# Reading a K and V cache in rows 64 KB apart: two successive loads share an 8 MB region and take alternate 32 KB pieces

## The chip, the core and the metric

The kernel runs on one core of a Trainium2 chip; the other cores are idle. The metric is device time in microseconds (us), lower is better. Executions of one kernel agree within about 0.3%. A verdict needs a difference of 2% outside a 95% interval. All ratios below are the mean time of one kernel's fast runs over that of the other's in the same rounds, so they are not quite the ratio of the medians quoted beside them.

## The reference, cut to what matters

One token attends to a cache of 65536 keys in each of 32 heads; a small gated MLP on the same token is mixed in. The two caches are 512 MB each (32 x 65536 x 128 x 2 bytes), so reading them is nearly all there is to do.

```python
H, Sk, Dh = 32, 65536, 128                 # x is [1, 1, 512], everything bf16
q = (x @ wq).reshape(1, 1, H, Dh)...       # one query per head
scores = einsum("bhqd,bhkd->bhqk", q, k_cache) * Dh ** -0.5
p = softmax(scores, axis=-1)
o = einsum("bhqk,bhkd->bhqd", p, v_cache)
a = o... @ wo
return g * a + (1 - g) * b                 # b: the MLP, g: a gate
```

The order of the keys within a head is of no account, as long as K and V agree on it: softmax and the sum over the keys do not see it.

## The kernel before

A load ("job") brings 4 MB: a quarter of one head's keys, 128 partitions with 128 keys (32 KB) each. There is a ring of four such slots in SBUF. K loads and V loads alternate in it. The SP engine issues every load as soon as the slot that it goes to is free.

```python
P = 128; CB_MAX = 128; NSLOT = 4           # CB = 128 keys per partition and load, NCH = 4 loads per head
ring = sb("ring", [P, NSLOT, SLOT], BF16)  # SLOT = 128 * 128 elements = 32 KB per partition

def kv_src(t, i):                          # the DRAM side of K or V load i
    h, c = divmod(i, NCH)
    return t[0, h, c * CB * P:(c + 1) * CB * P, :].rearrange("(p r) d -> p (r d)", p=P)

def pieces(job):
    ...
    src = kv_src(A_k_cache if kind == "k" else A_v_cache, i)
    dst = flat(job)[:, 0:CB * 128]
    ...
    return [(dst, src)]

def load(eng, w, job):                     # on SP, in the order of `jobs`
    i = place[job]
    if i >= NSLOT:
        for cond in free_of(jobs[i - NSLOT]):
            w(*cond)                       # the slot's old content is used up
    for n, (dst, src) in enumerate(pieces(job)):
        ...
        eng.dma_start(dst, src).then_inc(done, 16)
```

On the compute side each K load is transposed by PE (into psT) and copied by ScalarE (into KT), PE multiplies it with the query, and VectorE does a quarter of the keys itself (prod). Each V load goes to PE as weights. None of this is touched by the change.

## Time and profile before

| | before |
|---|---|
| time, median of the first 3 runs | 2563.17 us |
| bytes read | 1087.64 MB |
| PE / VectorE / ScalarE busy | 72% / 49% / 58% |
| DMA queue of the cache loads, share of 16 engines' span | 98.8% |

The lines below are from the page of the profile. The first two are the busy share of the 16 DMA engines and the rate in 40 equal slices of the span; then comes the queue that carries the loads (packets, MB, share of the engines' time), the chain of work that ended last, two groups that use the data (busy time and mean ns of one, then idle time before them and what ended it), and the loads with their size and the median time from issue to landing.

```profile
DMA  9999999999999999999999999999999999999996
GB/s 403 423 425 432 432 431 431 430 431 430 433 430 432 430 431 433 430 433 429 433 429 431 433 426 431 430 432 427 426 425 418 431 429 427 423 422 426 422 419 297
...
q1 hardware_dynamic: 37874, 1083.46, 98.8%
...
DMA ring<-in_A_k_cache_dram 66%; ACT KT L345 10%; PE psT L535 9%; PE psS L548 2%; PE psO L566 1%; ACT pcol L325 1%; DMA ring<-in_A_wq_dram 1%; PE psT L596 0%; PE psT L515 0%; POOL amx L304 0%; PE psS L508 0%; PE psO L589 0%; DVE mxs L441 0%; ACTq L205 0%; DVE sS L434 0%
...
L535 PE MATMUL psT<-ident,ring 128*128 128x128 bf16 x12288 | 1138.7, 255 | 527.6 <-DMA ring<-in_A_k_cache_dram 525.5
...
L424 DVE TENSOR_TENSOR prod<-ring,qbc 128x2048 f32<-128x2048 bf16 x256 | 586.7, 2292 | 592.1 <-DMA ring<-in_A_k_cache_dram 586.7
...
ring<-in_A_k_cache_dram SPq DMA_DIRECT2D x128, 4096.0 KB, 28.0
ring<-in_A_v_cache_dram SPq DMA_DIRECT2D x127, 4096.0 KB, 33.7
```

Reading: the DMA engines are busy in every slice but the last. PE and VectorE each sit idle for over 500 us, nearly all of it ended by a K load that landed. The chain is 66% K load. A load takes 28 to 34 us to land, although 4 MB at 431 GB/s take 9.7 us: about three loads stand in the queue at any time.

The SP queue's own waits (engine and line, what it waited for, us in total, times, longest) say who frees the slots:

```profile
SPq L205 <- DVE prod L424: 1368.2, 128, 11.8
SPq L252 <- PE psT L535: 522.0, 126, 10.7
SPq L252 <- PE psO L566: 487.1, 124, 7.3
```

SP waits 2377 us in these three lines, but for room in a queue that already holds work, so these waits cost nothing as long as the engines do not run dry.

The trace has a record of each packet. A packet here is one contiguous piece: one partition's row.

| packet | count | median ns | mean ns | us per engine, sum |
|---|---|---|---|---|
| 32 KB (K and V rows, and 128 of wq) | 32768 | 1214 | 1223.8 | 2506.4 |
| 14 KB (MLP weights) | 384 | 541 | 542.7 | 13.0 |
| 1 KB (nearly all wo) | 4097 | 46 | 50.4 | 12.9 |
| all others | | | | 15.0 |
| sum, of a span of 2563.3 us | | | | 2547.3 |

The last column is the time of all packets of that size divided by 16. It explains the time: 2547 of 2563 us are packets, so the 16 engines have next to no gaps between them. (A record does not name the engine of its packet, so this is the mean of the 16.) The fastest three quarters of the 32 KB packets lie between 1211 and 1218 ns, a rate of 27.0 GB/s per engine and 432 GB/s for 16.

### The profile page before, as it was taken

The page shows a single profiled execution, that of the slowest core. Times are in us where ns is not written, and L with a number is a line of the kernel's source. Part 1 is how long each engine was busy: PE and PEld are TensorE (multiplying, and loading weights), DVE is VectorE, ACT ScalarE, POOL GpSimd, SP SyncE. Part 2 cuts the span into 40 slices and gives each one's busy share as a digit, 9 for nine tenths or more (in the row PEclk, how much of TensorE's full clock was granted, in tenths as well). Part 3 has the DMA queues.
Part 4 walks back from the last instruction along what each step waited for, and adds up shares of the span by engine and source line. Part 5 has one row for each costly group of instructions (what it writes and reads, how often), then busy time and mean ns, then how long its engine had stood idle before and what let it go on. Part 6 is the DMA issues. An engine that isn't in the chain of part 4 may idle for free.

```text
span 2563.3 us, 88371 instructions
## 1 busy us (share of the span) xinstructions
PE 1848.0 (72%) x41279; PEld 1701.2 (66%) x41280; DVE 1259.2 (49%) x953; ACT 1484.7 (58%) x1799; POOL 42.3 (2%) x72
## 2 busy tenths in 40 slices
PE   6877777777777767776777677777766776777766
PEld 4777666666666666666766666666666666666665
DVE  2754554554455445544554454455444544455441
ACT  3766665566556655655665566556655665566552
POOL 0000000000000000000000000000000000000000
PEclk8778776777767767777676677777777777777776
DMA  9999999999999999999999999999999999999996
GB/s 403 423 425 432 432 431 431 430 431 430 433 430 432 430 431 433 430 433 429 433 429 431 433 426 431 430 432 427 426 425 418 431 429 427 423 422 426 422 419 297
DMA packets 42053, 1088.43 MB, mean 425 GB/s; under 512 B 4481, under 2 KB 8578, under 8 KB 8706
## 3 DMA queue, kind: packets, MB, share of 16 engines
q1 hardware_dynamic: 37874, 1083.46, 98.8%
q10 hardware_dynamic: 4112, 4.19, 0.5%
q8 instruction: 27, 0.44, 0.1%
q14 instruction: 40, 0.33, 0.0%
HBM read 1087.64 MB, written 0.00 MB: 424 GB/s over the span
## 4 chain that ended last, share of the span: by engine, by line
DMA 67%; PE 13%; ACT 11%; issue 9%; POOL 0%; DVE 0%; ACTq 0%; SPq 0%; POOLq 0%; DVEq 0%
DMA ring<-in_A_k_cache_dram 66%; ACT KT L345 10%; PE psT L535 9%; PE psS L548 2%; PE psO L566 1%; ACT pcol L325 1%; DMA ring<-in_A_wq_dram 1%; PE psT L596 0%; PE psT L515 0%; POOL amx L304 0%; PE psS L508 0%; PE psO L589 0%; DVE mxs L441 0%; ACTq L205 0%; DVE sS L434 0%
## 5 line engine op out<-in xcount | busy, mean ns | idle before, releaser
L345 ACT ACTIVATE KT<-psT 128x1024 bf16<-128x1024 bf16 x1536 | 1443.0, 1039 | 972.7 <-PE psT L535 969.8
L535 PE MATMUL psT<-ident,ring 128*128 128x128 bf16 x12288 | 1138.7, 255 | 527.6 <-DMA ring<-in_A_k_cache_dram 525.5
L535 PEld LDWEIGHTS psT<-ident,ring 128*128 128x128 bf16 x12288 | 912.3, 116 | 538.3 <-DMA ring<-in_A_k_cache_dram 271.7
L424 DVE TENSOR_TENSOR prod<-ring,qbc 128x2048 f32<-128x2048 bf16 x256 | 586.7, 2292 | 592.1 <-DMA ring<-in_A_k_cache_dram 586.7
L548 PE MATMUL psS<-qc,KT 128*128 128x1 bf16 x12288 | 550.8, 166 | 139.9 <-ACT KT L345 92.7
L548 PEld LDWEIGHTS psS<-qc,KT 128*128 128x128 bf16 x12288 | 467.7, 100 | 257.7 <-ACT KT L345 252.5
L426 DVE TENSOR_REDUCE sS<-prod 128x16 f32<-128x2048 f32 x256 | 585.2, 2286 | 8.7
L566 PE MATMUL psO<-pcol,ring 128*128 128x1 bf16 x16384 | 475.7, 164 | 19.9 <-issue 9.2
L566 PEld LDWEIGHTS psO<-pcol,ring 128*128 128x128 bf16 x16384 | 450.4, 99 | 24.0 <-issue 14.6
L434 DVE COPY sS<-psS 128x96 f32<-128x96 f32 x128 | 33.0, 257 | 607.2 <-PE psS L548 607.2
L325 ACT ACTIVATE pcol<-sS,nbias 128x128 bf16<-128x128 f32 x128 | 52.3, 408 | 41.7 <-POOL nbias L306 41.6
L304 POOL PARTITION_ALL_REDUCE amx<-mxs x32 | 16.1, 502 | 2137.5 <-DVE mxs L441 2137.5
L445 DVE COPY oparts<-psO 128x1 f32<-128x1 f32 x127 | 18.9, 149 | 25.2 <-PE psO L566 25.1
L306 POOL TENSOR_SCALAR nbias<-amx 128x1 f32<-128x1 f32 x32 | 24.5, 767 | 333.6 <-issue 333.6
L325 ACT ACTIVATION_READ_ACCUMULATOR pcol<-sS,nbias 128x1 f32 x128 | 26.1, 204 | 0.0
L380 DVE COPY qc<-qTb 128x1 bf16<-128x1 bf16 x128 | 19.9, 156 | 4.4
L441 DVE TENSOR_REDUCE mxs<-sS 128x1 f32<-128x512 f32 x32 | 21.7, 677 | 0.0
L332 ACT ACTIVATE qbc<-psT 128x512 bf16<-128x512 f32 x4 | 2.4, 597 | 23.1 <-PE psT L515 23.1
L596 PE MATMUL psT<-wo_sb,oTn 128*1 128x512 bf16 x31 | 11.2, 540 | 5.6 <-DVE oTn L476 5.6
L508 PE MATMUL psS<-xT,ring 128*128 128x1 bf16 x128 | 3.6, 165 | 12.3 <-DMA ring<-in_A_wq_dram 12.3
L508 PEld LDWEIGHTS psS<-xT,ring 128*128 128x128 bf16 x128 | 3.5, 104 | 12.4 <-issue 12.4
L596 PEld LDWEIGHTS psT<-wo_sb,oTn 128*1 128x1 bf16 x31 | 3.3, 110 | 12.7 <-issue 11.7
(44 smaller groups left out, 43.2 us busy)
## 6 DMA issues: line engine op xcount, KB each, us to landing
ring<-in_A_k_cache_dram SPq DMA_DIRECT2D x128, 4096.0 KB, 28.0
ring<-in_A_v_cache_dram SPq DMA_DIRECT2D x127, 4096.0 KB, 33.7
wo_sb<-in_A_wo_dram ACTq DMA_DIRECT2D x1, 4096.0 KB, 157.0
ring<-in_A_wq_dram SPq DMA_DIRECT2D x1, 4096.0 KB, 17.6
ring<-in_A_v_cache_dram SPq DMA_DIRECT2D x1, 3584.0 KB, 34.6
ring<-in_B_w_gate_dram SPq DMA_DIRECT2D x1, 1792.0 KB, 31.3
ring<-in_B_w_up_dram SPq DMA_DIRECT2D x1, 1792.0 KB, 35.5
ring<-in_B_w_down_dram SPq DMA_DIRECT2D x1, 1792.0 KB, 39.7
```

The source lines that it names most:

```text
L306: nc.gpsimd.tensor_scalar_mul(nbias[:, h:h + 1], amx[:, h:h + 1], -SCALE).then_inc(sm["s_nb"], 1)
L325: nc.scalar.activation(p_of(c), sS[:, h % NS, j * CB:(j + 1) * CB], ACT.Exp, bias=nbias[:, h:h + 1], scale=SCALE, accum_out=rsum[:, c:c + ...
L345: nc.scalar.activation(KT[:, g % NKT, :], kt_ps(g), ACT.Copy, bias=0.0).then_inc(sm[ev_of(g)[0]], 1)
L380: nc.vector.tensor_copy(qc[:, c % 2:c % 2 + 1], qTb[:, c // NCH:c // NCH + 1]).then_inc(sm[cq_of(c)[0]], 1)
L424: nc.vector.tensor_tensor(prod[:], kb, qb, ALU.mult).then_inc(sm["s_tt"], 1)
L426: nc.vector.reduce_sum(sS[:, h % NS, cc * CB + b0:cc * CB + b0 + DB], prod[:], AX_X).then_inc(sm["s_rd"], 1)
L434: nc.vector.tensor_copy(sS[:, h % NS, cc * CB:cc * CB + CBT], psS[:, c % 2, 0:CBT]).then_inc(sm["s_rc"], 1)
L441: nc.vector.reduce_max(mxs[:, h:h + 1], sS[:, h % NS, :], AX_X).then_inc(sm["s_mx"], 1)
L445: nc.vector.tensor_copy(oparts[:, c:c + 1], psO[:, c % 2, 0:1]).then_inc(sm[oc_of(c)[0]], 1)
L535: last = nc.tensor.transpose(dst[:, k * 128:(k + 1) * 128], src[:, b * 128:(b + 1) * 128], ident[:])
L548: last = mm(psS[:, c % 2, col:col + 1], KT[:, g % NKT, k * 128:(k + 1) * 128], qc[:, c % 2:c % 2 + 1], start=True, stop=True)
L566: last = mm(psO[:, c % 2, 0:1], src[:, b * 128:(b + 1) * 128], p_of(c)[:, b:b + 1], start=(b == 0), stop=(b == CB - 1))
```

## The change

The intent is to read the cache in another order in memory. Two successive loads share a region of 8 MB; partition p owns 64 KB of it and the even load takes the first 32 KB, the odd one the second. A row is still one contiguous piece of 32 KB, but rows of one load are now 64 KB apart in place of 32 KB.

```diff
         def kv_src(t, i):
             h, c = divmod(i, NCH)
-            return t[0, h, c * CB * P:(c + 1) * CB * P, :].rearrange("(p r) d -> p (r d)", p=P)
+            keys = t[0, h, c // 2 * 2 * CB * P:(c // 2 + 1) * 2 * CB * P, :]
+            return keys.rearrange("(p r) d -> p (r d)", p=P)[:, c % 2 * CB * 128:(c % 2 + 1) * CB * 128]
```

## The prediction

> **What bounds the kernel now.** The DMA engines. The profile's page gives them a busy digit of 9 in 39 of 40 slices, and a mean of 425 GB/s over a span of 2563.3 us. The compute engines are all below: PE 72%, ACT 58%, DVE 49%. The chain of waits that ended last is 66% "ring<-in_A_k_cache_dram". The SP queue's own waits show that it issues a load as soon as a slot is freed, and the issue table gives 28.0 us (K) and 33.7 us (V) from issue to landing for 4096 KB, about three times the 9.7 us that 4096 KB take at 431 GB/s: about three loads stand in the DMA queue all the time, so no engine waits for an issue. The packet records of the trace have 32768 packets of 32 KB, exactly 128 for each of 256 cache loads. Their median is 1213 ns, the first percentile too, so one engine runs at 27.0 GB/s and 16 at 432 GB/s: this is a floor of the engine, not of HBM waits. The mean is 1222.6 ns, because about 2% of the packets are slow (up to 3454 ns). The slow ones lie mostly after 1800 us, where the stretches table shows 420 to 428 GB/s in place of 431.
>
> **What the change does.** Only the source pattern of the K and V loads: a partition's 32 KB row is still one contiguous piece, but the pitch from partition to partition goes from 32 KB to 64 KB. Two successive loads then read the two halves of one 8 MB region. The built programs have the same instructions in the same order on each engine (1855 rows compared, no difference but line numbers); sizes, semaphores, slots and destinations are the same. Keys land in other columns, for K and V alike, so the softmax and the sum see the same pairs. Nothing is removed, nothing added: packets, bytes, issue costs and compute stay.
>
> **What can differ.** Only how fast HBM answers. The Trainium skill, "DMA: Bandwidth & Descriptors", section "Latency and other measured facts", reports for HBM copies of 16 KiB rows a loss at large power-of-two pitches: 207 against 214 GB/s at 512 KiB, 164 at 2 MiB. No run here shows this yet. 64 KB is an eighth of the pitch that cost 3% there, so I estimate a loss of a few tenths of a per cent at most, in a higher share of slow packets. The gain is bounded: if every packet took 1213 ns, 2048 packets per engine would save 2048 x 9.6 ns = 20 us, so about 2543 us (estimate). A gain over 2% is excluded by the engine floor: 1087.6 MB at 432 GB/s are 2517 us before head and tail.
>
> All of any packet slowdown lies on the critical path: 1% on the mean packet is about 25 us.
>
> **Prediction.** 2566 us, 8 in 10 between 2548 and 2595. Faster by over 2%: 0.01. Within 2%: 0.89. Slower by over 2%: 0.10.
>
> **What would show each step right or wrong.** Right: packet median still 1213 ns and 32768 packets of 32 KB; GB/s digits about 430 in the middle slices; landing times 28 and 34 us; unchanged counts and means in the groups of instructions. Wrong: a packet median above 1213 ns, or many more packets above 1300 ns, GB/s below 422 in the middle, with landing times up in proportion and longer PE and DVE waits for "ring<-in_A_k_cache_dram".
>
> **What would make it wrong.** Engines that read at the same time now stand twice as far apart in address; if that maps them on the same part of HBM, packets stretch and the time follows one for one (5% on the packet is 125 us). Or the slow packets after 1800 us come from the old addresses and vanish: then up to 20 us faster.

## The result, and the profile after

| | before | after |
|---|---|---|
| time, median of 4 runs each | 2563.11 us (2558.77 to 2563.19) | 2561.61 us (2560.03 to 2562.92) |
| ratio, 95% interval | | 0.9998 (0.9981 to 1.0015) |
| 32 KB packets: count, median, mean ns | 32768, 1214, 1223.8 | 32768, 1213, 1223.2 |
| 32 KB packets over 1400 ns | 424 | 386 |
| packet time per engine, of the span | 2547.3 of 2563.3 us | 2545.8 of 2560.1 us |

The change does nothing to the time. The same lines of the page, after:

```profile
DMA  9999999999999999999999999999999999999996
GB/s 403 423 427 430 432 431 433 430 432 430 431 431 431 432 430 431 433 430 430 433 430 431 431 429 429 428 428 429 430 427 425 433 426 427 422 425 429 425 425 297
...
q1 hardware_dynamic: 37874, 1083.46, 98.8%
...
DMA ring<-in_A_k_cache_dram 66%; PE psT L536 10%; ACT KT L346 10%; PE psS L549 2%; PE psO L567 1%; ACT pcol L326 1%; DMA ring<-in_A_wq_dram 1%; PE psT L597 0%; PE psT L516 0%; POOL amx L305 0%; PE psS L509 0%; PE psO L590 0%; DVE mxs L442 0%; ACTq L206 0%; DVE sS L435 0%
...
L536 PE MATMUL psT<-ident,ring 128*128 128x128 bf16 x12288 | 1143.2, 255 | 529.8 <-DMA ring<-in_A_k_cache_dram 527.9
...
L425 DVE TENSOR_TENSOR prod<-ring,qbc 128x2048 f32<-128x2048 bf16 x256 | 586.7, 2292 | 594.3 <-DMA ring<-in_A_k_cache_dram 589.0
...
ring<-in_A_k_cache_dram SPq DMA_DIRECT2D x128, 4096.0 KB, 28.0
ring<-in_A_v_cache_dram SPq DMA_DIRECT2D x127, 4096.0 KB, 33.7
```

Landing times are the same to a tenth of a us, the packet count is the same, the chain is the same 66%, and VectorE still waits 589 us for K loads (586.7 before).

### The profile page after: what moved, and what is told of

Its sections match the earlier page's. It is cut to its first block, busy times and chain, and to the rows that moved or that the text cites. A ratio compares the mean times of both kernels' runs of the same rounds, so it can differ in the third digit from the quotient of the medians.

```text
span 2560.1 us, 88371 instructions
## 1 busy us (share of the span) xinstructions
PE 1850.6 (72%) x41279; PEld 1704.9 (67%) x41280; DVE 1259.3 (49%) x953; ACT 1484.3 (58%) x1799; POOL 46.1 (2%) x72
## 4 chain that ended last, share of the span: by engine, by line
DMA 67%; PE 14%; ACT 11%; issue 9%; POOL 0%; DVE 0%; ACTq 0%; SPq 0%; POOLq 0%; DVEq 0%
DMA ring<-in_A_k_cache_dram 66%; PE psT L536 10%; ACT KT L346 10%; PE psS L549 2%; PE psO L567 1%; ACT pcol L326 1%; DMA ring<-in_A_wq_dram 1%; PE psT L597 0%; PE psT L516 0%; POOL amx L305 0%; PE psS L509 0%; PE psO L590 0%; DVE mxs L442 0%; ACTq L206 0%; DVE sS L435 0%
## 5 line engine op out<-in xcount | busy, mean ns | idle before, releaser
L425 DVE TENSOR_TENSOR prod<-ring,qbc 128x2048 f32<-128x2048 bf16 x256 | 586.7, 2292 | 594.3 <-DMA ring<-in_A_k_cache_dram 589.0
## 6 DMA issues: line engine op xcount, KB each, us to landing
ring<-in_A_v_cache_dram SPq DMA_DIRECT2D x127, 4096.0 KB, 33.7
```

The costliest lines, as they stand in the source:

```text
L425: nc.vector.tensor_tensor(prod[:], kb, qb, ALU.mult).then_inc(sm["s_tt"], 1)
```

## The experiments

A null result leaves three explanations, and the prediction had taken the first.

- **Engine floor.** A DMA engine moves 32 KB in 1213 ns, whatever the addresses; the memory has room to spare. The order in memory then does not matter until it is bad enough to eat up that room.
- **Memory order matters, but 64 KB is too small a step to show it.** A larger pitch then costs little by little.
- **The loads do not bound the kernel.** If slots or engines set the pace, faster or slower packets would be hidden.

Twelve kernels were run, each beside the kernel before on the same chip. Several read the wrong keys; the work done is the same. The comparison with the reference is of no use for seeing which keys were read.

### Fewer bytes with the same work: bytes_7_8

```diff
+            if place[job] >= 12:
+                return [(dst[:, 0:CB * 112], src[:, 0:CB * 112])]
             return [(dst, src)]
```

> From the 13th load on, each K and V load brings 7/8 of its row (28 KB in place of 32 KB); wrong result on purpose, all other work unchanged. DMA-bound theory: about 245 loads shrink by 1/8 of 9.75 us, 299 us less, so 2264 us within 1%. Rival (the engines' work or the release of slots bounds, and the memory pattern is masked by it): well under half of that gain, over 2410 us.

Measured: 2271.7 us, ratio 0.8877 (0.8855 to 0.8899). By the ratio that is 11.23% of the 2562 us that before took beside it (mean of seven runs), 288 us less. 246 loads shrank: the issue table has 121 K and 126 V loads of 3584 KB, but one of the V entries is the first piece of the last load, which is cut in two in every kernel (lines below). 246 x 8 rows per engine x the 152 ns between the median 32 KB packet of before (1214) and the median 28 KB packet of this run (1062) are 299 us. The loads bound the kernel: 96% of their saving arrives. The third explanation is out. The chain of waits and its waiting engines show where the rest goes (the issue table and the chain from the page, then the table of who waited for whom):

```profile
ring<-in_A_v_cache_dram SPq DMA_DIRECT2D x126, 3584.0 KB, 27.4
ring<-in_A_k_cache_dram SPq DMA_DIRECT2D x121, 3584.0 KB, 23.0
...
DMA ring<-in_A_k_cache_dram 37%; ACT KT L347 14%; PE psT L537 12%; PE psO L568 7%; PE psS L550 4%; ACT pcol L327 1%; POOL amx L306 1%; DMA ring<-in_A_wq_dram 1%; DVE mxs L443 1%; PE psT L598 0%; PE psT L517 0%; POOL nbias L308 0%; DVE sS L436 0%; PE psS L510 0%; PE psO L591 0%
```

```profile
DVE prod L426 <- DMA ring<-in_A_k_cache_dram: 215.5, 97, 3.7
PE psT L537 <- DMA ring<-in_A_k_cache_dram: 169.8, 88, 3.9
```

K loads fall from 66% to 37% of the chain, VectorE's waits for them from 586.7 to 215.5 us, and PE is busy for 82% of the span in place of 72%. There is not much room behind the DMA.

### A larger pitch: pitch128k, pitch512k, pitch2m, pitch4m

These widen the region that a load is spread over. At 128 KB the four loads of a head share it and the result is right. At 512 KB, 2 MB and 4 MB, 4, 16 and all 32 heads share it, and keys of different heads are mixed. Where the texts below say "the skill", they mean the row of the page that the prediction names, and the times that they work out from its figures are estimates.

```diff
-            return t[0, h, c * CB * P:(c + 1) * CB * P, :].rearrange("(p r) d -> p (r d)", p=P)
+            # pitch128k
+            keys = t[0, h].rearrange("(p r) d -> p (r d)", p=P)
+            return keys[:, c * CB * 128:(c + 1) * CB * 128]
+            # pitch512k; pitch2m has 16 heads and 64 loads in place of 4 and 16
+            g = h // 4 * 4
+            keys = t[0, g:g + 4].rearrange("h s d -> (h s) d").rearrange("(p r) d -> p (r d)", p=P)
+            n = i % 16
+            return keys[:, n * CB * 128:(n + 1) * CB * 128]
+            # pitch4m
+            keys = t[0].rearrange("h s d -> (h s) d").rearrange("(p r) d -> p (r d)", p=P)
+            return keys[:, i * CB * 128:(i + 1) * CB * 128]
```

> The change taken one step further: the four loads of a head share its 16 MB, rows 128 KB apart; the result stays right. Engine theory (a DMA engine moves 32 KB in 1213 ns whatever the addresses): packet median 1213 ns, time 2561 us within 0.3%. Memory-order theory (the pitch costs, but 64 KB is too little to show it): some loss here, 1% or more (over 2585 us).

> The largest pitch that the cache allows: rows of one load stand 4 MB apart, loads step by 32 KB. The result is wrong on purpose (keys of different heads are mixed), the work is the same. Engine theory in its pure form: 2561 us within 0.3%. Memory-order theory, with the skill's halving of HBM copies at a 4 MiB pitch: the packet mean doubles, 4000 us or more. In between if the memory has some headroom at this pitch.

> Rows of a load 512 KB apart (four heads share 64 MB; wrong result on purpose). Theory of engines in step (16 engines that read at the same offset modulo the pitch meet on the same part of the memory, and the pitch has to be large): a small loss between nothing (pitch128k) and 7.3% (pitch4m), estimate 0 to 2%, 2561 to 2612 us, packet median still 1213 ns. The skill's table of HBM copies would give 3% here, 2640 us. Theory that pitch4m is slow for another reason than a power-of-two pitch (rows of 16 or more heads touched by each load): no loss here.

> Rows 2 MB apart (16 heads share 256 MB; wrong result on purpose). Engines in step: between pitch512k and pitch4m, 2580 to 2750 us, with the slowest slices at the start, where the engines have not drifted apart yet. The skill's table for copies (164 against 214 GB/s) would give 30%, 3300 us.

| pitch | time, median us | ratio to before (95%) | packet median / mean ns | packets over 1400 ns |
|---|---|---|---|---|
| 32 KB (before) | 2563.11 | | 1214 / 1223.8 | 424 |
| 64 KB (the change) | 2561.61 | 0.9998 (0.9981 to 1.0015) | 1213 / 1223.2 | 386 |
| 128 KB | 2562.07 | 1.0003 (0.9985 to 1.0022) | 1214 / 1222.2 | 325 |
| 512 KB | 2562.28 | 1.0000 (0.9983 to 1.0016) | 1214 / 1222.3 | 381 |
| 2 MB | 2567.74 | 1.0026 (1.0009 to 1.0043) | 1213 / 1224.1 | 499 |
| 4 MB | 2757.30 | 1.0730 (1.0702 to 1.0757) | 1213 / 1299.7 | 4782 |

Kernels are compared only within the same rounds. Of the six runs of pitch4m, two (2822 and 2779 us) count as slow, being over 1.5% above the fastest; the ratio is of the other four. Their granted clocks (0.720 and 0.717) are hardly below those of the others (0.719 to 0.723), so the spread may well be this kernel's own; the mean of all six is 7.9% above the 2562 us of before. The second explanation, loss little by little, does not hold in the range of the change: up to 512 KB nothing is lost, at 4 MB 7.3%. At 2 MB it is 0.26%: the interval leaves out 1, but the mean packet of the profiled run (1224.1 ns against 1223.8) hardly shows it. The pure form of the first falls as well: an engine's packet is not independent of the addresses everywhere. At 4 MB the median packet is still 1213 ns, but one packet in seven (4782 of 32768) is over 1400 ns. The excess over 1213 ns, summed and divided by 16, grows from 22 to 178 us per engine, so 155 of the 161 us that the span of the profiled run is longer (2724.3 against 2563.3 us).

The Trainium skill, "DMA: Bandwidth & Descriptors", section "Latency and other measured facts", gives for copies between HBM tensors in 16 KiB rows 207 GB/s at a pitch of 512 KiB, 164 at 2 MiB and 103 at 4 MiB, of 214. The direction agrees, the sizes do not carry over to these loads from HBM into SBUF in 32 KB rows: 0%, 0.26% and 7.3% more time here, against 3%, 23% and 52% less rate there.

### The same distance, another remainder: pitch4m_skew

```diff
+            pitch = H * S - P * CB               # in keys: 128 partitions, each 4 MB less 32 KB
+            keys = t[0].rearrange("h s d -> (h s) d")[0:pitch, :].rearrange("(p r) d -> p (r d)", p=P)
+            n = i % (NK - 1)
+            return keys[:, n * CB * 128:(n + 1) * CB * 128]
```

> As pitch4m, but a row stands 4 MB less 32 KB after the one before it: as much memory touched by each load, rows as far apart, but no longer at the same offset modulo 4 MB (wrong result on purpose). Engines in step: the loss goes, 2561 us within 0.5%, packet mean 1223 ns, first slices 403 and 423 GB/s as before. Theory that distance or the spread over 512 MB costs: 7% slower as pitch4m, 2750 us.

Measured: 2561.01 us, ratio 0.9999 (0.9982 to 1.0015). The rates by slice, first pitch4m, then pitch4m_skew:

```profile
GB/s 313 290 334 381 396 398 395 423 421 420 405 401 419 426 417 403 418 426 427 420 406 409 414 411 414 410 425 427 419 406 392 410 411 410 398 403 420 427 387 249
```

```profile
GB/s 403 422 428 433 430 431 432 433 428 433 433 427 433 432 427 433 433 428 433 430 430 433 430 429 431 431 430 431 426 424 432 429 425 427 415 429 431 425 431 299
```

With 32 KB taken off the pitch the whole loss is gone: packet mean 1222.3 ns, 324 packets over 1400 ns. So it is neither the distance between rows nor the spread over 512 MB that costs, but that the rows of a load lie at the same remainder modulo 4 MB. (A pitch of 2 MB also gives equal remainders, modulo 2 MB, and costs 0.26%; why 4 MB costs so much more was not tested.) This agrees with the skill's advice in the same row of its table to pad such a pitch by a few KiB (it tells of +4 KiB; here it was -32 KB).

### The same bytes for all: one_row and hot4m

```diff
+            # one_row: every partition reads the same 32 KB
+            row = t[0, h, c * CB * P:c * CB * P + CB, :].rearrange("r d -> (r d)")
+            return row.unsqueeze(0).broadcast_to([P, CB * 128])
+            # hot4m: every load reads the first 4 MB of K or of V
+            return t[0, 0, 0:CB * P, :].rearrange("(p r) d -> p (r d)", p=P)
```

> All 128 partitions of a load are filled from the same 32 KB row (pitch 0; wrong result on purpose). Engine theory in its pure form (an engine's rate needs nothing of the memory): 2561 us. Engines in step: 16 engines want the same bytes at the same time, at least the loss of pitch4m, over 2750 us, unless the memory serves repeated rows from something faster.

> All 256 cache loads read the same 4 MB of K or of V; wrong result on purpose. Theory that the slow packets (over 1400 ns; 424 in before, 386 in after) are a matter of addresses: they mostly go, excess over 1213 ns falls from 22 us to under 10 us, time 2545 to 2552 us. Theory that they come from what the program does at that moment: the same clusters once per head after 1600 us, 2561 us within 0.2%.

one_row: 2560.77 us, ratio 0.9997 (0.9980 to 1.0013), with a wrong result. My expectation of a loss was wrong: 128 rows at one address do no harm, while 128 different rows 4 MB apart do. Whether repeated rows come from something faster was not looked into.

hot4m: 2562.83 us, ratio 1.0008 (0.9988 to 1.0028), 370 packets over 1400 ns and 20.4 us of excess, against 424 and 22.1 before. So the slow packets are not a matter of which addresses are read, as the last sentence of the prediction had held possible. The records say more: after 1600 us many of them come in clusters, in all three kernels of this table at nearly the same moments. (Counting as a cluster five or more slow packets less than 3 us from one to the next, 247 of the 424 of before lie in clusters, some of them earlier. The times below are on the clock of the records; the span of the profile's other tables starts at 11 us on it, so subtract 11.)

| kernel | some clusters of slow packets, us |
|---|---|
| before | 1750, 1830, 1909, 1989, 2066, 2145 |
| after | 1752, 1830, 1909, 1986, 2065, 2144 |
| hot4m | 1751, 1829, 1908, 2066, 2146 |

### Once per head, or once per eight loads: loads2m

```diff
-CB_MAX = 128
+CB_MAX = 64
```

> The kernel before with loads of half the size (2 MB, rows of 16 KB), so 16 loads to a head in place of 8. The result stays right. Where do the slow packets come from, which all kernels so far show every 8 loads, 78 us, after 1600 us? If they belong to the DMA queue (a count of loads): every 8 loads, so about every 39 us. If they belong to the program (something done once per head): every 16 loads, 78 us. Time: 8 ns more for each of 2048 extra packets per engine (the packet records give 46 ns for 1 KB, 159 for 4 KB, 309 for 8 KB, so about 8 ns fixed), 16 us more, 2578 us within 1%.

Measured: 2593.45 us, ratio 1.0122 (1.0105 to 1.0139). Clusters at 1782, 1862, 1942, 2101 and 2181 us: one in 80 us, that is 16 loads, not 8. With bytes_7_8, where a head takes less time, they are 70 us apart, still one per head. So they belong to something that the program does once per head, and not to a count of loads in the DMA queue. What that is was not found; all of it together is at most the 22 us of excess, 0.9%. The time is 0.6% above the 2578 us that were expected (32 us more than before, not 16): the slices of the first 130 us are slow (361 and 320 GB/s), with slots of half the size.

### Smaller pieces: piece2k

```diff
+            keys = t[0, h, c // 2 * 2 * CB * P:(c // 2 + 1) * 2 * CB * P, :]
+            keys = keys.rearrange("(p n two r) d -> p n two (r d)", p=P, two=2, r=8)
+            return keys[:, :, c % 2, :]
...
-            dst = flat(job)[:, 0:CB * 128]
+            dst = flat(job)[:, 0:CB * 128].rearrange("p (n x) -> p n x", x=1024)
...
-                cut = (CB - TAIL) * 128
+                cut = (CB - TAIL) // 8
```

> The change with smaller pieces: two slots share the 8 MB region and take alternate 2 KB of each partition's 64 KB, in place of alternate 32 KB. The result stays right. Engine theory (about 8 ns fixed and 37.6 ns per KB for each packet, from the packets of 1, 4 and 8 KB in the trace of before): 2 KB take 84 ns, 32 KB 1340 ns in place of 1213, so 2048 x 127 ns = 260 us more, 2821 us within 2%. Memory theory (the same bytes within 8 MB in another order, served alike): 2561 us.

Measured: 2834.72 us, ratio 1.1068 (1.1049 to 1.1086); expected were 2821 us within 2%. The page's queue line:

```profile
q1 hardware_dynamic: 529266, 1083.46, 103.9%
```

524288 packets of 2 KB have a median of 88 ns, and their times overlap a little (103.9%), so the rate is the safer number: 386 GB/s in the middle slices, against 431. The result is right and the region is the 8 MB of the change; only the length of a piece differs. It is the contiguous length that has a price here, about 9 ns for each further packet (273 us for 15 x 2048 of them per engine), and the change kept that length.

### Who meets whom at 4 MB: pitch4m_stagger and pitch4m_stagger2

Rows at the same remainder may clash between engines that work in step, or within one engine's own sequence of rows. Slow first slices in pitch4m (313, 290, 334, then around 400 and over) looked like engines that start in step and drift apart. To build a stagger from the start, 15 small loads of 15, 14, ... 1 rows were added to pitch4m, meant to give some engines more to do than others; how the rows of a load are shared among the engines is not in the records.

```diff
+            for job in jobs[:2]:                 # pitch4m_stagger2 only
+                load(sp, w, job)
+            at = 0
+            for n in range(15, 0, -1):
+                sp.dma_start(KT[at:at + n, 0, :], A_k_cache[0, 0, 0:n * GB, :].rearrange(
+                    "(p r) d -> p (r d)", p=n)).then_inc(sm["s_junk"], 16)
+                at += n
-            for job in jobs:
+            for job in jobs[2:]:                 # pitch4m_stagger: jobs
                 load(sp, w, job)
...
                 w("tdone", g + 1)
+                w("s_junk", 240)                 # ScalarE, before it writes KT
```

> As pitch4m (wrong result on purpose), but 15 small loads of 15, 14, ... 1 rows of 2 KB go into the queue first[...]; the addresses of the cache loads are those of pitch4m. Theory of engines in step (different engines meet on the same part of the memory): with the engines apart from the start, the first 250 us run at over 390 GB/s in place of 275 to 335, and the loss shrinks from 7.3% to under 3%, under 2640 us (the small loads themselves cost about 8 us). Theory that one engine's own successive rows clash, or that distance costs: same slow start, 2750 us.

> pitch4m_stagger again, mended: there the small loads went into an empty queue, one every 0.48 us, while 2 KB take 0.084 us, so the engines had caught up before the next one and the stagger was never built. Here they are issued behind wq and the first K load, into a full queue (about 20 us of work, 7.2 us of issue)[...] (wrong result on purpose, addresses of pitch4m). Engines in step: from the second K load on over 390 GB/s, which the stretches from 100 to 250 us show in place of 275 to 335; loss under 4%, under 2660 us. One engine's own rows: the same slow start, 2690 to 2760 us. In pitch4m_stagger, with no stagger, the loss was 5.8%, so a loss between 4% and 6% in total decides nothing; the first 250 us decide.

pitch4m_stagger took 2700.99 us, ratio 1.0580 (1.0525 to 1.0636), but tells nothing: it put the small loads into an empty queue, 0.48 us apart (15 in 7.19 us of issue), while 2 KB take under 0.1 us. No stagger came about. pitch4m_stagger2 put them behind wq and the first K load: 2690.81 us, ratio 1.0541 (1.0467 to 1.0616). The stretches decide (us, busy us of each engine with counts, granted clock, DMA share, GB/s), first pitch4m, then pitch4m_stagger2:

```profile
100.00:150.00 50.00, 37.55 (x704) 34.98 (x704) 29.22 (x19) 34.53 (x40) 0.64 (x2) 0.70 0.99 299
150.00:200.00 50.00, 26.34 (x530) 24.71 (x531) 18.79 (x11) 23.36 (x28) 0.00 (x0) 0.64 0.99 335
200.00:250.00 50.00, 30.84 (x728) 28.34 (x726) 20.16 (x17) 23.06 (x29) 0.64 (x2) 0.70 1.01 377
```

```profile
100.00:150.00 50.00, 32.50 (x655) 29.38 (x653) 25.17 (x18) 31.33 (x37) 0.64 (x2) 0.74 0.96 324
150.00:200.00 50.00, 28.88 (x640) 26.89 (x640) 19.86 (x15) 23.16 (x28) 0.38 (x1) 0.67 1.00 346
200.00:250.00 50.00, 31.49 (x677) 28.77 (x678) 22.37 (x16) 25.16 (x31) 1.61 (x1) 0.70 0.99 376
```

The rates are 299, 335, 377 and 324, 346, 376 GB/s: a little better at first, far from the 390 that engines in step required; pitch4m_stagger, with small loads but no stagger, had 298, 313 and 343. The drift theory did not pass its test. It is not refuted either: in pitch4m_stagger2 the 120 small packets ran from 32.2 to 37.8 us, the last four one at a time, so not all engines left them together, but the records do not name the engine of a packet, so I cannot show that the stagger was as meant or lasted. The three kernels ran on three different chips. The load of wo (4 MB in packets of 1 KB, on the other DMA queue) does not explain the slow start by itself: it landed after 261 us in pitch4m, but after 129 us in pitch4m_stagger, which was still at 313 GB/s from 150 to 200 us, and after 182 us in pitch4m_skew, which ran at 421 to 430. One rival was not tested: load i reads at the remainder i x 32 KB, so in all three kernels the slow start is also the stretch of the lowest remainders. Which rows meet stays open.

No experiment points to a kernel that beats both. The bytes are fixed, the packets run at the engines' rate, and a wholly even stream would save the 22 us of excess at most.

## Why the prediction was right

- **What bounds the kernel.** Right, and shown by bytes_7_8: 96% of the time taken from the loads is gone from the total. Two figures in the text were slightly off: the median of the packets before is 1214 ns and not 1213, the mean 1223.8 and not 1222.6. Its 2% of slow packets fits its own later limit of 1300 ns (577 of 32768); over 1400 ns are 1.3%. And 128 of the 32768 are rows of wq, the last V load being cut in two. With the right mean the bound on the gain is 2048 x 10.8 ns = 22 us, not 20.
- **Nothing is removed or added.** Right: same packets, same groups, same landing times (28.0 and 33.7 us).
- **A loss of a few tenths of a per cent at most, in more slow packets.** The bound held, but the sign did not show: 386 slow packets against 424, ratio 0.9998. The step rested on the skill's 3% at 512 KiB, measured on copies from HBM to HBM; pitch512k shows no loss at all at that pitch for loads into SBUF, at 2 MB it is 0.26%, and the first clear loss is that at 4 MB. The term was sized too large: it is zero here. The 2566 us predicted is 0.2% above the 2561.61 measured.
- **"A floor of the engine, not of HBM waits."** Right for the addresses of the change and up to 512 KB, where the packet does not move: 1213 or 1214 ns at four pitches, and for one row read 128 times. At a pitch of 4 MB, where only the addresses read differ, the mean packet is 1299.7 ns, so 1213 ns is not the time of a packet for every choice of addresses. So the null result is a margin that was not used up, not a law.
- **"Or the slow packets after 1800 us come from the old addresses and vanish."** It was held possible and is wrong. They stay when the same 4 MB are read all the time (hot4m), and their clusters come once per head, whatever the size of a load.

## What to carry to other kernels

When a stream of contiguous 32 KB rows already runs at the DMA engines' own rate, do not expect a gain from rearranging where in memory the rows lie (none here, at pitches from 32 KB to 4 MB): first compare the median packet with its fastest, and only the difference of the mean (here 11 ns in 1224) is to be had. What does cost is the length of the contiguous piece (2 KB pieces: 10.7%) and a pitch of a very large power of two (4 MB: 7.3%), and the second went away when the pitch was moved off it by one row. Before testing such a change, take it to its extreme: one run at 4 MB told more than the run at 64 KB could.

## What the Trainium skill lacked or had wrong

- "DMA: Bandwidth & Descriptors", "Latency and other measured facts": the table of row pitches is of copies between HBM tensors. For loads from HBM into SBUF, 32 KB rows, one core: no loss at 64, 128 and 512 KB (ratios 0.9998, 1.0003, 1.0000), 0.26% at 2 MB, 7.3% at 4 MB; 4 MB less 32 KB restores the full rate (0.9999).
- The same place offers lock-stepped streams as an unverified inference for the loss. Small loads meant to stagger the engines' start did not restore the rate (324 to 376 GB/s from 100 to 250 us), though a lasting stagger was not shown, and 128 partitions that read one and the same row lost nothing (0.9997); so that inference remains unverified.
- The same page, "Specifications", has 512 B as the least transfer for line rate. Pieces of 2 KB ran at 386 GB/s against 431 with 32 KB; the packets of 1, 4 and 8 KB (46, 159 and 309 ns) give about 8 ns fixed for each packet.
- The same page, "Where 436 GB/s comes from", puts the ceiling of 16 engines at 435.2 GB/s. Nothing is lacking there, the trace agrees within 1%: the fastest packets are 1211 to 1213 ns for 32 KB, 432 GB/s for 16 engines.
- No page tells of slow packets (up to 3454 ns in place of 1213) in clusters at a fixed point of the program, here once per head; some 22 us of excess per engine in 2563 us. Their cause was not found.
